# Block 0's second layer by unit halves, w_out in two transfers, and the transposing transfers one pair sooner in SyncE's queue

## The chip, the cores and the metric

The kernel runs on one core of a Trainium2 chip. The core has five engines with a queue of instructions each: PE (TensorE, matrix products and transposes), DVE (VectorE), ACT (ScalarE), POOL (GpSimd) and SP (SyncE, which here only issues transfers). Each queue is worked off in order, and an instruction that waits holds all that stand behind it. Sixteen DMA engines move data between HBM and SBUF. Matrix results land in PSUM, in eight banks. The metric is the time of one execution on the device in microseconds (us); lower is better. Shown are the median over several executions, and the profile of one of them.

## The reference

The input x has four sequences of 6144 tokens with 256 features. First a gated recurrence runs along each sequence, for each feature by itself:

```
f = lower_bound + (1 - lower_bound) * sigmoid(f_logit)
h[t] = f[t] * h[t-1] + (1 - f[t]) * x[t]
```

Then a layer works on each of the 24576 tokens, with the recurrence's output as its input h:

```
out = maximum(h @ w1, h @ w2) @ w_out        # w1, w2: 256 x 1024, w_out: 1024 x 256
```

All arrays are float32 outside. Inside, the kernel computes in float16 with float32 sums.

## The kernel before, in words

**What is computed.** With wd = w2 - w1 the maximum is h @ w1 + relu(h @ wd). So the first layer needs only h @ wd and a ReLU (`first_layer`, L434 and L442), and the part h @ w1 @ w_out is folded into one 256 x 256 matrix w13 = w1 @ w_out (`make_w13`, L390). The recurrence is run with u = 1 - sigmoid (ACT), and the factor 1 - lower_bound is folded into the weights. The second layer (`second_layer`, L480) sums ten products per group of 128 tokens: two with w13 and eight with w_out's 1024 units. From pair 2 on, two blocks are computed together by a scheme with seven products in place of eight (`sevenths`, L643), whose sums and differences DVE forms (L499), and whose results leave PSUM by ACT (L559) and DVE (L561) into the tile osb, and from there by SyncE's `store` to memory.

**Tiles and stages.** A block is 512 tokens. The first four blocks are chunks 0 to 3 by themselves; every later chunk has 1024 tokens and is a pair of blocks, so chunk c (c from 4) is pair c - 2, and the last is pair 23. The opening prepares the weights and blocks 0 to 3; then one loop runs over the pairs, sixteen slots each. In a slot TensorE computes one of a pair's sixteen first-layer units (two products of 512 columns) and nine or so products of the pair before. ACT and DVE meanwhile run the sigmoid (`pair_gate`, L279), the decay (L207), the product with x (L217) and the scan (L224) of the pair after.

**How a chunk comes in.** Features must lie on the partitions, and the types must be float16. `fetch` (POOL, L100) casts f_logit and x of a chunk from memory into a scratch array in memory, of which there are two for each. `cross` lets SyncE transpose them from scratch into SBUF (tiles fT and xT, four buffers each, L148), then lets POOL wait until fT has landed, with a copy of one element into `waited` (`pool_waits`, L341), and then fetches the next chunk. So cast, transpose, POOL's wait and the next cast follow one another. Blocks 0 to 3 come in without scratch and are transposed by TensorE (`first_turn`, L136; `turn`, L174).

**What sets the order.** The schedule is written out by hand: each engine's queue holds the instructions in the order in which the program makes them. In the opening, POOL's queue is: a wait for the first part of w1, the transfer of w_out into the tile wob (L666), then the inputs of chunks 1 to 4. TensorE's is: block 0's first layer, `make_w13`, the turning of block 1, and block 0's second layer in seven of eight slots with the turning of block 2 and the first layer of block 1 between. `cross(4)` stands before block 0's second layer, `cross(5)` behind block 1's, and in the loop, at slot 2 of pair p, stands the `cross` of pair p + 2. SyncE's queue therefore holds the transposes of chunk c, then the two stores of pair c - 5, then the transposes of chunk c + 1. The tile osb has four buffers, two per pair. PSUM has two double banks for the first layer (tile dT) and four for all else (tile ps).

In the profile, chunk 4's transposes are issued at 25.74 and 28.20 us, and the first product of pair 2 starts at 44.83 us.

Of the kernel before, what the change touches and what calls it, by code (L numbers as in the profile page):

```python
# [18 lines left out]
def kernel(  # L19
# [295 lines left out]
    lbr = const.tile([KC, P], FP32)  # L315
    waited = const.tile([P, 1], FP32)
    warm = const.tile([P, 1], FP32)
    wob = wpool.tile([P, FC, D], HALF)
    wd = wpool.tile([P, KC, DFF], HALF)
    w1T = wpool.tile([P, FC, D], HALF)  # L320
    w13 = wpool.tile([P, KC, D], HALF)
# [18 lines left out]
    def pool_waits(t):  # L340
        nc.gpsimd.tensor_copy(out=waited[:], in_=t)  # L341

    def scale_w1(g):
        for kc in range(KC):
            nc.scalar.mul(w1s[g][:, kc, :], w1n[g][:, kc, :], om[:, kc : kc + 1])

    def half_w1(g, copy):
        for kc in range(KC):
# [20 lines left out]
        g, q = divmod(fc, NQ)  # L369
        return slice(g * NQ * P + q, (g + 1) * NQ * P, NQ)  # L370

    def turn_w1(g):
        pt = ps_o.tile([P, NQ, KC, P], HALF, name="ps")
        for q in range(NQ):
            for kc in range(KC):
                nc.tensor.transpose(
                    pt[:, q, kc, :], w1h[g][:, kc, q : NQ * P : NQ], ident[:]
                )
        return pt
# [5 lines left out]
        )  # L385

    def make_w13(kc):
        psw = ps_o.tile([P, 2, D], FP32, name="ps")
        for fc in range(FC):
            nc.tensor.matmul(  # L390
                psw[:, 0, :],
                lhsT=w1T[:, fc, kc * P : (kc + 1) * P],
                rhs=wob[:, fc, :],
                start=(fc == 0),
                stop=(fc == FC - 1),
            )
        nc.scalar.copy(out=w13[:, kc, :], in_=psw[:, 0, :])

# [1 line left out]

    def right(k, cols):

        return wob[:, k * KH : (k + 1) * KH, cols], w13[:, k, cols]

    def make_sevens():
        b11, b12, b21, b22 = (right(k, c) for k in range(2) for c in (lo, hi))
# [19 lines left out]
    def first_layer(j, fc):  # L428
        k, g = divmod(fc, KH)
        if fc % 2 == 0:  # L430
            dts["d"] = ps_d.tile([P, 2, TB], FP32, name="dT")
        dT = dts["d"]
        for kc in range(KC):
            nc.tensor.matmul(  # L434
                dT[:, fc % 2, :],
                lhsT=wd[:, kc, unit_cols(fc)],
                rhs=y_of(j, kc),
                start=(kc == 0),
                stop=(kc == KC - 1),
            )  # L440
        if fc % 2:
            nc.scalar.activation(  # L442
                out=rts[j, k][:, g - 1 : g + 1, :].rearrange(
                    "p q (i m) -> p q i m", m=P
                ),
                in_=dT[:].rearrange("p q (m i) -> p q i m", m=P),
                func=AF.Relu,
            )

    def store(j, osb, groups=slice(0, TB // P), cols=slice(0, D), queue=None):  # L450
        b, t0, nb, c, o = blocks[j]
        r0 = b * S + t0
        (queue or nc.sync).dma_start(
            out=out[r0 : r0 + nb, :].rearrange("(p n) d -> p n d", p=P)[
                :, groups, cols
            ],
            in_=osb[:, groups, cols],
        )
# [3 lines left out]
    def second_layer(j, slot):  # L462
        ns = TB // P
        n = KC + FC
        total = ns * n
        for k in range(slot * total // FC, (slot + 1) * total // FC):
            i, s = divmod(k, n)
            g, r = divmod(i, 2)
            if s == 0 and r == 0:
                acc["ps"] = ps_o.tile([P, 2, D], FP32, name="ps")  # L470
                if i == 0:
                    acc["osb"] = opool.tile([P, TB // P, D], FP32, name="osb")
            ps, osb = acc["ps"], acc["osb"]
            toks = slice(i * P, (i + 1) * P)
            if s < KC:
                left, right = y_of(j, s)[:, i:TB:ns], w13[:, s, :]
            else:
                fc = s - KC
                left, right = rts[j, fc // KH][:, fc % KH, toks], wob[:, fc, :]
            nc.tensor.matmul(  # L480
                ps[:, r, :],
                lhsT=left,
                rhs=right,
                start=(s == 0 and r == 0),
                stop=(s == n - 1 and r == 1),
                skip_group_check=True,
            )
            if r == 1 and s == n - 1:
                (nc.scalar.copy if j in (0, 3) else nc.vector.tensor_copy)(
                    out=osb[:, 2 * g : 2 * g + 2, :], in_=ps[:]  # L490
                )
                if i == ns - 1:
                    store(j, osb)

    sums = {}

# [160 lines left out]
    with tc.manual_schedule():  # L657
# [4 lines left out]
        fetch_first(1)  # L662
        for g in range(NG):
            fetch_w(g)
        pool_waits(w1n[0][:, 0, 0:1])
        nc.gpsimd.dma_start(  # L666
            out=wob[:].rearrange("p (g q) c -> p g (q c)", g=NG),
            in_=moe_w_out.rearrange("(g p q) c -> p g (q c)", g=NG, q=NQ),
        )
        for c in range(1, 5):  # L670
            for s in range(2):
                fetch(c, s)
        wt = ps_d.tile([P, 2, 2 * TB], HALF, name="dT")
        lbc = ps_d.tile([P, TB], FP32, name="dT")

# [21 lines left out]
        first_turn(1, 0)  # L697
        first_turn(1, 1)
        first_recurrence(1)
        warm_up(24)  # L700
        scale_w1(0)
        half_w1(0, nc.scalar.copy)
        scale_w1(1)
        pt0 = turn_w1(0)
        for pair in range(2):
            make_wd(0, pair)
            for fc in range(2 * pair, 2 * pair + 2):
                first_layer(0, fc)
        half_w1(1, nc.vector.tensor_copy)
        pt1 = turn_w1(1)  # L710
        for pair in range(2):
            make_wd(1, pair)
            for fc in range(4 + 2 * pair, 6 + 2 * pair):
                first_layer(0, fc)
        keep_w1T(0, pt0)
        keep_w1T(1, pt1)
        steps = turn_steps(1)
        make_w13(0)
        turn(steps[:8])
        gate(1)  # L720
        make_w13(1)
        turn(steps[8:])
        for step in scan_steps(1):
            step()
        cross(4)
        for fc in range(FC):
            if fc == 4:
                turn(turn_steps(2))
                gate(2)
            if fc == 6:  # L730
                first_layer(1, 0)
                first_layer(1, 1)
            if fc < 7:
                second_layer(0, fc)
        for step in scan_steps(2):
            step()
        for step in make_sevens():
            step()
        for fc in range(2, FC):
            first_layer(1, fc)  # L740
            if fc == 3:
                second_layer(0, 7)
        turn(turn_steps(3))
        gate(3)
        early = scan_steps(3)
        for fc in range(FC):
            first_layer(2, fc)
            second_layer(1, fc)
            if fc < 4:
                early[fc]()  # L750
        cross(5)
        scans = {PAIR0: pair_scans(PAIR0)}
        gates = {0: 0, 1: 1, 4: 2, 5: 3}
        order = {
# [16 lines left out]
        for p in range(PAIR0, NPAIR):  # L771
            first = p == PAIR0
            more = p + 1 < NPAIR
            seq = [
                (27, scans[p]["scan10"]),
                (36, scans[p]["scan11"]),
                (112, lambda: sum3(p)),
            ]
            if more:
                scans[p + 1] = pair_scans(p + 1)  # L780
                seq += [
                    (64, scans[p + 1]["decay0"]),
                    (66, scans[p + 1]["drive0"]),
                    (70, scans[p + 1]["scan00"]),
                    (84, scans[p + 1]["scan01"]),
                    (131, scans[p + 1]["decay1"]),
                    (133, scans[p + 1]["drive1"]),
                ]
            if not first:
                seq += [  # L790
                    (9, lambda: sum1(p - 1)),
                    (18, lambda: sum2(p - 1)),
                    (50, lambda: sum4(p - 1)),
                ]
                queue += sevenths(p - 1)
            seq.sort(key=lambda e: e[0])
            gates = {4: 0, 6: 1, 12: 2, 14: 3} if more else {}
            for slot in range(2 * FC):
                first_layer(2 * p + slot // FC, slot % FC)
                if first and slot in pieces3 or p == PAIR0 + 1 and slot == 1:  # L800
                    second_layer(2 * PAIR0 - 1, piece)
                    piece += 1
                if p > PAIR0 + 1 or (p == PAIR0 + 1 and slot >= LAG):
                    due += NSEV / (2 * FC)
                    while due >= 1:
                        due -= 1
                        queue.pop(0)()
                if slot == 2 and p + 2 < NPAIR:
                    cross(blocks[2 * p + 4][3])
                if slot in gates:  # L810
                    pair_gate(p + 1, gates[slot])
                while seq and seq[0][0] < (slot + 1) * 9:
                    seq.pop(0)[1]()
# [38 lines left out]
```

## Time and profile before

| What | Before |
|---|---|
| Median of 4 executions | 380.51 us (378.33 to 380.92) |
| The profiled execution: its time, and its span in the profile | 380.78 us, 379.0 us |
| PE busy | 369.8 us, 98% of the span |
| DVE, ACT, POOL busy | 338.5, 303.2, 44.1 us |
| Granted TensorE clock | full throughout |
| Bytes moved | 77.17 MB, mean 204 GB/s |
| Cast into scratch: f, x, from issue to landing | 7.8, 10.2 us (median of 22 each) |
| Transposes of f, x, from issue to landing | 6.2, 5.0 us (median of 22 each) |
| Stores of 512 KB, from issue to landing | 4.4 us (median of 46) |

The busy shares say how much of the span an engine worked; matrix products overlap, so a busy PE is not one at its peak. The profile also gives the chain of work that ended last, followed back from the last instruction, and for each group of instructions the idle time of its engine just ahead, with what ended it. In the timeline a row is: start in us, length in us, engine (a q behind it is the engine's own sequencer, which issues transfers or waits), line, operation, output and inputs, count, and in brackets the idle time ahead and what ended it. In the windows a row has, for each engine, busy us and the number of instructions, then the TensorE clock, the DMA share and GB/s.

### The profile page before, as it was taken

What the parts mean: (1) busy time and instruction counts of PE and PEld (TensorE: products, weight loads), DVE (VectorE), ACT (ScalarE), POOL (GpSimd) and SP (SyncE); (2) the same over time, 40 slices, a digit from 0 to 9 for tenths busy, and PEclk for the clock granted to TensorE, in tenths of its full rate; (3) what the DMA queues carried; (4) which work ended last, traced back from release to release, by engine and by line L of the source; (5) the groups of instructions that cost most, each with busy time, mean ns of one, the idle gap of its engine ahead of it and who ended that gap; (6) DMA issues with size and microseconds to landing.
All of it is one profiled execution on the core that took longest, in us unless ns stands there. A gap on an engine that the chain in (4) does not pass through costs nothing.

```text
span 379.0 us, 9634 instructions
## 1 busy us (share of the span) xinstructions
PE 369.8 (98%) x4156; PEld 281.9 (74%) x4156; DVE 338.5 (89%) x408; ACT 303.2 (80%) x412; POOL 44.1 (12%) x80
## 2 busy tenths in 40 slices
PE   7899999999999999999999999999999999999995
PEld 6577767777777777777777777777777777777784
DVE  5796789999999999999999999999999899999762
ACT  4956798888888798888888888887987788889752
POOL 1501102102101011012012011010210110200000
PEclk9999999999999999999999999999999999999999
DMA  8999989999989899999999998997998988993223
GB/s 279 205 204 256 199 159 256 219 183 265 223 151 246 133 252 214 191 198 312 158 212 175 236 259 164 237 254 126 277 194 162 258 174 216 280 141 140 113 110 114
DMA packets 104543, 77.17 MB, mean 204 GB/s; under 512 B 93298, under 2 KB 95348, under 8 KB 103796
## 3 DMA queue, kind: packets, MB, share of 16 engines
q1 hardware_dynamic: 101536, 51.19, 59.0%
q0 software_dynamic: 2544, 25.17, 36.3%
q8 instruction: 32, 0.52, 0.6%
q10 hardware_dynamic: 420, 0.20, 0.2%
q14 instruction: 11, 0.09, 0.1%
HBM read 53.48 MB, written 48.23 MB: 268 GB/s over the span
## 4 chain that ended last, share of the span: by engine, by line
DMA 61%; PE 32%; POOL 2%; issue 2%; SPq 1%; ACT 1%; DVE 0%; POOLq 0%; DVEq 0%
DMA scr<-in_f_logit_dram 29%; DMA fT<-scr 28%; PE dT L434 14%; PE ps L643 13%; PE ps L480 5%; DMA xT<-in_x_dram 2%; POOL waited L341 2%; DMA r<-in_moe_w_dram 2%; PE ps L174 1%; SPq L117 0%; ACT r L442 0%; POOL wob L666 0%; DVE osb L561 0%; ACT u L279 0%; POOL fT L105 0%
## 5 line engine op out<-in xcount | busy, mean ns | idle before, releaser
L442 ACT ACTIVATE r<-dT 128x1024 f16<-128x1024 f32 x192 | 196.0, 1023 | 52.5 <-PE dT L434 52.3
L434 PE MATMUL dT<-r,wd 128*128 128x512 f16 x768 | 225.0, 379 | 0.7 <-ACT r L442 0.7
L643 PEld LDWEIGHTS <-S 128*128 128x128 f16 x1760 | 115.5, 101 | 37.2 <-DVE S L499 0.2
L643 PEld LDWEIGHTS <-r 128*128 128x128 f16 x1320 | 90.9, 101 | 36.9 <-issue 0.2
L224 DVE TENSOR_TENSOR_SCAN r<-ff,r,v 128x512 f16<-128x512 f16 x88 | 108.1, 1269 | 0.8
L643 PE MATMUL ps<-t,S 128*128 128x128 f16 x1320 | 101.6, 219 | 0.0
L499 DVE TENSOR_TENSOR S<-r 128x2560 f16<-128x2560 f16 x44 | 65.4, 1486 | 13.9 <-ACT r L442 13.9
L434 PEld LDWEIGHTS <-wd 128*128 128x128 f16 x768 | 67.7, 113 | 5.4 <-issue 0.8
L643 PE MATMUL ps<-wob,r 128*128 128x128 f16 x704 | 69.9, 219 | 0.0
L499 DVE TENSOR_TENSOR S<-r,S 128x2560 f16<-128x2560 f16 x44 | 64.9, 1474 | 0.0
L279 ACT ACTIVATE u<-fT 128x512 f16<-128x512 f16 x88 | 56.1, 638 | 1.8 <-DMA fT<-scr 1.8
L341 POOL CAST waited<-fT 128x1 f32<-128x1 f16 x22 | 18.3, 832 | 287.5 <-DMA fT<-scr 287.5
L207 DVE TENSOR_SCALAR ff<-u,nom 128x512 f16<-128x512 f16 (+1 forms) x98 | 31.8, 345 | 10.3 <-ACT u L279 4.4
L643 PE MATMUL ps<-w,r 128*128 128x128 f16 x176 | 38.5, 219 | 0.0
L643 PE MATMUL ps<-t,r 128*128 128x128 f16 x430 | 34.1, 219 | 0.1
L561 DVE TENSOR_TENSOR osb<-ps,sn 128x512 f32<-128x512 f32 x44 | 30.1, 684 | 3.2 <-PE ps L643 3.2
L643 PE MATMUL ps<-wob,S 128*128 128x128 f16 x352 | 32.6, 219 | 0.0
L217 DVE TENSOR_TENSOR v<-u,xT 128x1024 f16<-128x1024 f16 x44 | 30.1, 683 | 0.8 <-DMA xT<-scr 0.7
L549 ACT COPY sn<-ps 128x512 f32<-128x512 f32 x44 | 25.8, 587 | 2.0 <-PE ps L643 2.0
L559 ACT COPY osb<-ps 128x512 f32<-128x512 f32 x43 | 25.0, 582 | 0.8 <-PE ps L643 0.8
L480 PEld LDWEIGHTS <-r 128*128 128x128 f16 x160 | 16.0, 101 | 6.5
L643 PE MATMUL ps<-w,S 128*128 128x128 f16 x88 | 19.3, 219 | 0.0
(58 smaller groups left out, 136.3 us busy)
## 6 DMA issues: line engine op xcount, KB each, us to landing
out_dram<-osb SPq DMA_DIRECT2D x46, 512.0 KB, 4.4
scr<-in_f_logit_dram POOLq DMA_DIRECT2D x22, 512.0 KB, 7.8
scr<-in_x_dram POOLq DMA_DIRECT2D x22, 512.0 KB, 10.2
r<-in_moe_w_dram SPq DMA_DIRECT2D x4, 512.0 KB, 7.1
fT<-in_f_logit_dram POOLq DMA_DIRECT2D x3, 256.0 KB, 7.9
xT<-in_x_dram POOLq DMA_DIRECT2D x3, 256.0 KB, 8.7
out_dram<-osb SPq DMA_DIRECT2D x3, 256.0 KB, 2.5
osb<-in_f_logit_dram SPq DMA_DIRECT2D x2, 256.0 KB, 3.3
```

What stands on the lines that cost most here:

```text
L207: nc.vector.tensor_scalar(out=ff[:, h, cols], in0=u[:, h, cols], scalar1=nom[:, h : h + 1], scalar2=1.0, op0=ALU.mult, op1=ALU.add,)
L217: nc.vector.tensor_tensor(out=like(v[:, :, cols], xT), in0=like(u[:, :, cols], xT), in1=xT, op=ALU.mult,)
L224: nc.vector.tensor_tensor_scan(out=y_of(j, h), data0=ff[:, h, o : o + TB], data1=v[:, h, o : o + TB], initial=0.0 if t0 == 0 else y_of(j - ...
L279: nc.scalar.activation(out=mids[p + NBLK, "u"][:, h, cols], in_=held[c, 0][:, h, cols], func=AF.Sigmoid, scale=-1.0,)
L341: nc.gpsimd.tensor_copy(out=waited[:], in_=t)
L434: nc.tensor.matmul(dT[:, fc % 2, :], lhsT=wd[:, kc, unit_cols(fc)], rhs=y_of(j, kc), start=(kc == 0), stop=(kc == KC - 1),)
L442: nc.scalar.activation(out=rts[j, k][:, g - 1 : g + 1, :].rearrange("p q (i m) -> p q i m", m=P), in_=dT[:].rearrange("p q (m i) -> p q i ...
L480: nc.tensor.matmul(ps[:, r, :], lhsT=left, rhs=right, start=(s == 0 and r == 0), stop=(s == n - 1 and r == 1), skip_group_check=True,)
L499: nc.vector.tensor_tensor(out=t[:], in0=a, in1=b, op=op)
L549: nc.scalar.copy(out=t[:], in_=bank[b][:])
L561: nc.vector.tensor_tensor(out=dst, in0=bank[b][:], in1=snap[name][:], op=ALU.add)
L643: nc.tensor.matmul(bank[b][:, i, :], lhsT=a[:, k, cols], rhs=w, start=fresh, stop=after is not None, skip_group_check=True,)
```

## The change

There are two parts.

In the opening, w_out comes in two transfers into two tiles, one for each half of the 1024 units, and POOL's wait ahead of them is for block 0's last sigmoid. Block 0's second layer is split by unit halves (`second_first`): units 0 to 3 of all four token groups run right behind their first layer, ahead of the second half of w1's turning; the two terms with w13 and units 4 to 7 follow after `make_w13`. The second half of w1 is scaled by DVE in place of ACT. Block 0's last ReLU goes to DVE. w13's two halves share one PSUM tile of the first layer's pool. Block 2's transposes are split into those of f and those of x. Block 0's results leave by ACT as before, and block 3's too.

In the queue of SyncE, `cross` of each chunk from 5 on stands one block or pair sooner: `cross(5)` ahead of block 1's second layer, `cross(6)` behind it, and in the loop that of pair p + 3 at pair p. SyncE's queue then holds the transposes of chunk c and behind them the stores of pair c - 6.

```diff
-    wob = wpool.tile([P, FC, D], HALF)
+    wob = [wpool.tile([P, KH, D], HALF, name=f"wob{g}") for g in range(2)]
...
     def make_w13(kc):
-        psw = ps_o.tile([P, 2, D], FP32, name="ps")
+        if kc == 0:
+            dts["w"] = ps_d.tile([P, 2, TB], FP32, name="dT")
+        psw = dts["w"][:, kc, :]
...
+            if j == 0 and fc == FC - 1:
+                nc.vector.tensor_scalar_max(out=dst, in0=src, scalar1=0.0)
+            else:
+                nc.scalar.activation(out=dst, in_=src, func=AF.Relu)
...
+    def open_first():
+        acc["first"] = [ps_o.tile([P, 2, D], FP32, name="ps") for g in range(2)]
+        acc["osb0"] = opool.tile([P, TB // P, D], FP32, name="osb")
+
+    def second_first(i, fcs, y=False):
+        ns = TB // P
+        g, r = divmod(i, 2)
+        ps, osb = acc["first"][g], acc["osb0"]
+        toks = slice(i * P, (i + 1) * P)
+        terms = [(y_of(0, s)[:, i:TB:ns], w13[:, s, :]) for s in range(KC) if y]
+        terms += [
+            (rts[0, fc // KH][:, fc % KH, toks], wob[fc // KH][:, fc % KH, :])
+            for fc in fcs
+        ]
+        for n, (left, right) in enumerate(terms):
+            nc.tensor.matmul(
+                ps[:, r, :],
+                lhsT=left,
+                rhs=right,
+                start=(fcs[0] == 0 and r == 0 and n == 0),
+                stop=(fcs[-1] == FC - 1 and n == len(terms) - 1),
+                skip_group_check=True,
+            )
+        if fcs[-1] == FC - 1 and r == 1:
+            nc.scalar.copy(out=osb[:, 2 * g : 2 * g + 2, :], in_=ps[:])
+            if i == ns - 1:
+                store(0, osb)
...
-        pool_waits(w1n[0][:, 0, 0:1])
-        nc.gpsimd.dma_start(
-            out=wob[:].rearrange("p (g q) c -> p g (q c)", g=NG),
-            in_=moe_w_out.rearrange("(g p q) c -> p g (q c)", g=NG, q=NQ),
-        )
-        for c in range(1, 5):
-            for s in range(2):
-                fetch(c, s)
...
         first_recurrence(1)
+        pool_waits(mids[0, "u"][:, 0, TB - 1 : TB])
+        for g in range(NG):
+            nc.gpsimd.dma_start(
+                out=wob[g][:].rearrange("p q c -> p (q c)"),
+                in_=moe_w_out[g * NQ * P : (g + 1) * NQ * P, :].rearrange(
+                    "(p q) c -> p (q c)", q=NQ
+                ),
+            )
+        for c in range(1, 5):
+            for s in range(2):
+                fetch(c, s)
         warm_up(24)
-        scale_w1(0)
+        scale_w1(0, nc.scalar.mul)
         half_w1(0, nc.scalar.copy)
-        scale_w1(1)
         pt0 = turn_w1(0)
         for pair in range(2):
             make_wd(0, pair)
             for fc in range(2 * pair, 2 * pair + 2):
                 first_layer(0, fc)
+        keep_w1T(0, pt0)
+        scale_w1(1, nc.vector.tensor_scalar_mul)
         half_w1(1, nc.vector.tensor_copy)
-        pt1 = turn_w1(1)
+        pt1 = new_pt()
+        open_first()
+        for fcs in ((0, 1), (2, 3)):
+            for i in range(TB // P):
+                second_first(i, fcs)
+        turn_w1(1, pt1)
         for pair in range(2):
             make_wd(1, pair)
+            if pair:
+                keep_w1T(1, pt1)
             for fc in range(4 + 2 * pair, 6 + 2 * pair):
                 first_layer(0, fc)
-        keep_w1T(0, pt0)
-        keep_w1T(1, pt1)
         steps = turn_steps(1)
-        make_w13(0)
         turn(steps[:8])
         gate(1)
+        make_w13(0)
+        turn(steps[8:])
         make_w13(1)
-        turn(steps[8:])
         for step in scan_steps(1):
             step()
         cross(4)
-        for fc in range(FC):
-            if fc == 4:
-                turn(turn_steps(2))
-                gate(2)
-            if fc == 6:
-                first_layer(1, 0)
-                first_layer(1, 1)
-            if fc < 7:
-                second_layer(0, fc)
+        last = tuple(range(KH, FC))
+        for i in range(3):
+            second_first(i, last, True)
+        steps = turn_steps(2)
+        turn(steps[:8])
+        gate(2)
+        second_first(3, last, True)
+        first_layer(1, 0)
+        first_layer(1, 1)
+        turn(steps[8:])
         for step in scan_steps(2):
             step()
         for step in make_sevens():
             step()
         for fc in range(2, FC):
             first_layer(1, fc)
-            if fc == 3:
-                second_layer(0, 7)
         turn(turn_steps(3))
         gate(3)
+        cross(5)
         early = scan_steps(3)
         for fc in range(FC):
             first_layer(2, fc)
             second_layer(1, fc)
             if fc < 4:
                 early[fc]()
-        cross(5)
+        cross(6)
...
-                if slot == 2 and p + 2 < NPAIR:
-                    cross(blocks[2 * p + 4][3])
+                if slot == 2 and p + 3 < NPAIR:
+                    cross(blocks[2 * p + 6][3])
```

## The prediction

> **What bounds the kernel now.** I read the page's busy shares first, then the chain that ended last, then the queues of SP and POOL, then the opening microseconds.
>
> ```profile
> PE 369.8 (98%) x4156; PEld 281.9 (74%) x4156; DVE 338.5 (89%) x408; ACT 303.2 (80%) x412; POOL 44.1 (12%) x80
> ...
> DMA 61%; PE 32%; POOL 2%; issue 2%; SPq 1%; ACT 1%; DVE 0%; POOLq 0%; DVEq 0%
> DMA scr<-in_f_logit_dram 29%; DMA fT<-scr 28%; PE dT L434 14%; PE ps L643 13%; PE ps L480 5%; DMA xT<-in_x_dram 2%; POOL waited L341 2%; DMA r<-in_moe_w_dram 2%; PE ps L174 1%; SPq L117 0%; ACT r L442 0%; POOL wob L666 0%; DVE osb L561 0%; ACT u L279 0%; POOL fT L105 0%
> ```
>
> TensorE is busy 98% of the span, yet the chain runs through DMAs: cast f into scratch, transpose it into SBUF, let POOL see it, start the next cast. Both are true only if two bounds lie side by side. The waits of the SP queue and of POOL say that the DMA loop waits for nothing but itself:
>
> ```profile
> SPq L148 <- DMA scr<-in_f_logit_dram: 168.4, 21, 20.8
> ...
> POOL waited L341 <- DMA fT<-scr: 287.5, 22, 15.7
> ```
>
> The timeline of SP shows two turns of the loop:
>
> ```profile
> 79.13 4.12 SPq L148 DMA_TRANSPOSE fT<-scr  x1
> 83.34 2.85 SPq L148 DMA_TRANSPOSE xT<-scr  x1
> 86.30 1.51 SPq L453 DMA_DIRECT2D out_dram<-osb  x2
> 94.37 3.59 SPq L148 DMA_TRANSPOSE fT<-scr  x1
> 98.21 1.94 SPq L148 DMA_TRANSPOSE xT<-scr  x1
> 100.25 2.29 SPq L453 DMA_DIRECT2D out_dram<-osb  x2
> ```
>
> SP sits idle from 87.8 to 94.37, when the cast of chunk 9 lands. From chunk 8 (79.13) to chunk 25 (334.52) a turn takes 255.39/17 = 15.0 us. A pair of blocks takes TensorE 14.72 us (the sigmoids of successive chunks start at 74.68, 89.40, 104.12, 118.85). So the loop loses 0.3 us per pair against TensorE. In the trace the sigmoid of chunk 7 starts 3.1 us after its transpose landed, that of chunk 12 0.5 us, those of chunks 19 to 25 0.0 to 0.7 us. Once it costs TensorE something (timelines of ACT and PE):
>
> ```profile
> 287.45 0.58 ACT L559 COPY osb<-ps 128x512 f32<-128x512 f32 x1
> 297.14 0.63 ACT L279 ACTIVATE u<-fT 128x512 f16<-128x512 f16 x1 [1.52 <-DMA fT<-scr]
> 303.08 0.58 ACT L559 COPY osb<-ps 128x512 f32<-128x512 f32 x1
> ```
> ```profile
> 298.73 0.59 PE L434 MATMUL dT<-r,wd 128*128 128x512 f16 x2 [0.70 <-ACT r L442]
> ```
>
> The ReLU stands behind the late sigmoid on ACT. The two copies of successive pairs are 15.63 us apart instead of 14.72: 0.9 us lost, the one visible stall of the steady part. The opening is the other place (windows):
>
> ```profile
> 15.00:20.00 5.00, 4.15 (x43) 3.20 (x42) 2.10 (x5) 3.48 (x5) 0.49 (x1) 1.00 1.12 210
> 10.00:20.00 10.00, 8.51 (x76) 5.87 (x74) 6.63 (x16) 8.14 (x12) 4.97 (x9) 1.00 1.01 194
> ```
> ```profile
> 18.96 0.62 PE L174 MATMUL ps<-ident,xT 128*128 128x128 f16 x8 [0.85 <-DMA xT<-in_x_dram]
> ```
>
> TensorE idles 1.49 us of those ten, 0.85 us of it for block 1's x. From 20 us on it is full.
>
> **What the Trainium skill says.** "DMA: Bandwidth & Descriptors", section "Issuing engines are not separate DMA queues": DMAs of all issuers interleave on the same 16 engines. The trace agrees: a pair of stores issued before the next cast lands in 3.9 us (median, 251.2), a pair around its issue in 12.0 us:
>
> ```profile
> out_dram<-osb SPq DMA_DIRECT2D x2, 512.0 KB, 12.0
> scr<-in_f_logit_dram POOLq DMA_DIRECT2D x1, 512.0 KB, 8.9
> ```
>
> "SBUF — State Buffer", section "Who interferes with whom": a DVE operation in a 2-port mode locks GpSimd out; this touches the moved POOL wait and its DMA issues. The traced one-element POOL copies take 0.18 to 1.32 us, so something holds them. "VectorE: DVE Perf Modes", section "The perf-mode tier table": fp32 tensor_scalar in SBUF runs at 2x, PSUM fp32 at 1x.
>
> **Part 1, the opening.** The matmuls are the same (40 of 256 columns for block 0's second layer); only order and engines change. POOL now waits for block 0's second sigmoid (ends 7.82) instead of w1 (9.04). Copy 0.2 to 0.65; wob's issue starts near 8.4 instead of 9.63. Two issues at 0.55 (the fT row's price) replace one of 0.87: chunk 1's issue is about 1.0 us earlier, and the whole POOL stream with it. First half of wob: its packets then share the engines with the weights until about 12, so I put its landing at 13.3 (bounds 12.8 and 14.5).
>
> TensorE, from rows of the timeline (8 transposes 0.43, 8 matmuls of 256 columns 0.86, 8 of 512 1.71): first-layer units 0-3 end at 13.74 as now; the second ReLU ends at 14.85. Second layer with units 0-3, 16 matmuls, from 13.95 to 15.75. Second w1 half: DVE does wd (to 12.01), keep (0.64), two scalings (fp32 tensor_scalar, unseen; 0.43 like the fp32 cast, at most 0.68), two casts (0.86), so it is ready at 14.4 to 14.9, hidden behind those 16 matmuls. Transposes to 16.2, units 4-7 to 17.9. Then fT of block 1 to 18.3, w13 first half to 19.2, xT to 19.65 (x lands near 18 now: its wait is gone). But w13's halves now share one PSUM tile, and ACT has the sigmoid (1.02) before the first w13 copy: copy ends 19.8, second half to 20.7, copy to 21.15, and only then the second term of the remaining second layer. That is 0.2 + 0.4 us idle. The last ReLU on DVE (unseen; 1024 fp32 from PSUM, 1.2 us by the 1.22 us of the drive, bounds 1.0 to 1.4) ends at 19.2 and is hidden by w13. Remaining: 23 matmuls 2.46, block 2's transposes 0.86, block 1's first layer 3.41, block 3's transposes 0.86; ACT's ReLUs (1.02 each against 0.86 on TensorE) add about 0.5. Block 2's first layer starts near 29.4; the DVE chain gives 29.5. Now it starts at 28.97. So **+0.4 us**, bounds -1.5 (all opening idleness filled) and +1.2 (wob late).
>
> **Part 2, the queue.** SP's order becomes f, x of chunk c, then the stores of pair c-6 instead of c-5. The transposes wait for their casts, so moving them cannot start them sooner by itself. The chain gains only what no longer lies beside it: the earlier POOL stream (about 1.0 us, bounds 0 and 1.2); block 1's store at 37.77, now behind chunk 5's transposes (fT took 7.3 us to land, without it some 6: 1.3, plus 0.3 of SP's wait); at chunk 8 one store beside the loop instead of two (one turn with two took 14.7 us for cast and transpose, chunk 7's with one 11.3; I count 1.4). Sum g = 4.0 us of lead, bounds 1 and 6. Any g over 1.5 removes the 0.9 us stall: **-0.9 us**.
>
> The price is behind the waiting transposes: each store leaves one turn, 14.7 us, later, and holds its osb buffer; there are four, two per pair. The stores after chunk c's transposes must land before pair c-4 first writes. With today's landing times and g = 0 the worst is chunk 21: issued 280.33 and 280.95, landed 291.6 and 293.7, needed at 287.45 (ACT) and 288.99 (DVE): 4.1 and 4.7 us late. With g = 4 that is 0.1 and 0.7, within what ACT can absorb (at 297 an ACT gap of 1.52 cost TensorE 0.70, so about 0.8). All others are earlier. So **0**, bounds 0 and +3.9.
>
> The inp buffers add no wait: chunk c takes that of chunk c-4, whose last sigmoid ran more than 20 us before.
>
> Sum against the execution shown: 379.0 + 0.4 - 0.9 + 0 = 378.5 us span, 1.78 around it, 380.3 for its 380.78. The median of the runs is 380.51, so 380.0.
>
> **Rivals.**
> A (0.40), as summed: 380.0. Its own range is 378.7 to 382.3, within 0.5% (1.9 us, about what a measurement of this kernel can tell from no change).
>
> B (0.31), faster: the opening fills its 1.49 us idle and the chain's lead takes the 0.9 us, 380.5 - 2.4 = 378.1. For it: the four runs reach down to 378.33, so an undisturbed loop may be worth more than the one visible stall. Against: TensorE's sum above meets new waits at w13.
>
> C (0.22), slower: SyncE's stores come too late. With g = 1 the worst lateness is 3.7, less 0.8 absorbed, 2.9; with -0.9 + 0.4 it gives +2.4, 382.9, and 383.9 at g = 0. It decides below g = 1.5 or when stores land later than 12.7 us after issue. For it: in 9 of the 18 pairs of stores between 70 and 330 us at least one now takes over 10 us. Against: the lead of part 2.
>
> D (0.07): wob's first half lands at 14.5 or later, or POOL is held by DVE: TensorE waits at the first second-layer matmul, and the ACT order adds its share, +2 us, 382.5.
>
> That the transposes do not start sooner at all is contained in C: then g is the POOL stream alone.
>
> **The numbers.** Faster by over 0.5% 0.31 (B), within 0.40 (A), slower 0.29 (C, D). The range: 377.4 below B (0.7 for what the other runs suggest), 383.5 inside C.
>
> **What would show it.** Right: no ACT wait for fT after 100 us; fT landing 4 us or more ahead of its sigmoid; leave copies 14.72 apart throughout; block 2's first layer starting at 29 to 30; SP's stores about 14 us after their copies. Wrong: ACT or DVE at the leaves (L559, L561 of now) waiting for a store's DMA; a wait for wob at 14; the first f transpose not before 25.5; block 2's first layer before 28.3.

## The result, and the profile after

| | Before | After |
|---|---|---|
| Median | 378.95 us (64 runs, 377.93 to 382.73, and one of 429.01) | 380.13 us (43 runs, 379.31 to 381.79) |
| The profiled execution: time, span | 380.78 us, 379.0 us | 380.13 us, 378.4 us |
| PE busy | 369.8 us, 98% | 368.3 us, 97% |
| DVE, ACT, POOL busy | 338.5, 303.2, 44.1 us | 340.2, 301.0, 37.8 us |

The changed kernel takes 1.003 of the time before, 95% interval 1.002 to 1.0039: it is 1.2 us slower. The forecast time was 380.0, and 380.13 was measured; the forecast direction was wrong. The cause of that shows in the first row. The four runs shown ahead of the prediction had a median of 380.51 us. The 64 runs that the comparison now holds, those four among them, have 378.95, and only 9 of them lie at 380.2 or above, three of the four among these nine. In three later comparisons the same kernel had 378.87, 379.06 and 379.06.

The page of after, its busy shares, the chain that ended last by engine and by line, and the sigmoids:

```profile
PE 368.3 (97%) x4156; PEld 280.4 (74%) x4156; DVE 340.2 (90%) x411; ACT 301.0 (80%) x409; POOL 37.8 (10%) x81
...
PE 94%; DMA 3%; ACT 1%; SPq 0%; issue 0%; DVE 0%; POOL 0%; DVEq 0%
PE ps L677 45%; PE dT L439 43%; PE ps L484 3%; DMA wob<-in_moe_w_out_dram 2%; PE ps L516 1%; DMA osb<-in_x_dram 1%; PE ps L174 1%; SPq L117 0%; PE dT L395 0%; ACT r L452 0%; ACT u L201 0%; DVE osb L595 0%; ACT w L402 0%; ACT u L252 0%; DVE osb L616 0%
...
L279 ACT ACTIVATE u<-fT 128x512 f16<-128x512 f16 x88 | 56.0, 637 | 0.0
```

The chain has left the DMA loop: 94% of it is TensorE, where in the profile of before 61% was DMA. The 1.8 us that the sigmoids waited for fT are 0.0. But neither is the change's doing alone: two more profiles of the kernel before (below) have 94% and 96% of TensorE in the chain and no such wait. The page of the last of them:

```profile
PE 96%; DMA 1%; ACT 1%; SPq 0%; DVE 0%; issue 0%; DVEq 0%
```

The waits of the SP queue and of POOL (total us, times, longest) nevertheless look almost as they did (168.4 and 287.5 before):

```profile
SPq L148 <- DMA scr<-in_f_logit_dram: 167.6, 22, 20.3
...
POOL waited L341 <- DMA fT<-scr: 278.4, 22, 16.5
```

So the size of these two waits does not tell what sets the end; the loop now runs ahead of TensorE. The timeline of SP after, chunks 8 and 9:

```profile
76.72 4.43 SPq L148 DMA_TRANSPOSE fT<-scr  x1
81.25 2.08 SPq L148 DMA_TRANSPOSE xT<-scr  x1
83.44 0.99 SPq L457 DMA_DIRECT2D out_dram<-osb  x2
91.79 2.82 SPq L148 DMA_TRANSPOSE fT<-scr  x1
94.71 2.81 SPq L148 DMA_TRANSPOSE xT<-scr  x1
97.62 0.99 SPq L457 DMA_DIRECT2D out_dram<-osb  x2
```

Chunk 8's transpose is issued at 76.72 instead of 79.13, and chunk 25's at 318.69 instead of 334.52, so that a turn of the loop takes (318.69 - 76.72)/17 = 14.2 us instead of 15.0. Its lead over TensorE, the time from the landing of a chunk's fT to the first sigmoid that reads it, grows from 6.1 us at chunk 8 to 12 to 14 us at the end. The leave copies of the place where before lost 0.9 us (timeline of ACT after) are 14.72 apart again:

```profile
287.72 0.58 ACT L593 COPY osb<-ps 128x512 f32<-128x512 f32 x1
...
302.44 0.58 ACT L593 COPY osb<-ps 128x512 f32<-128x512 f32 x1
```

The loss is in the opening, as the experiments below show. Its timeline on TensorE:

```profile
13.75 1.91 PE L516 MATMUL ps<-wob,r 128*128 128x256 f16 x16 [0.48 <-DMA wob<-in_moe_w_out_dram]
...
18.11 1.04 PE L395 MATMUL dT<-wob,w1T 128*128 128x256 f16 x8
18.99 0.61 PE L174 MATMUL ps<-ident,xT 128*128 128x128 f16 x8
19.65 1.03 PE L395 MATMUL dT<-wob,w1T 128*128 128x256 f16 x8
20.52 0.27 PE L516 MATMUL ps<-w,r 128*128 128x256 f16 x1
21.14 0.27 PE L516 MATMUL ps<-w,r 128*128 128x256 f16 x1 [0.35 <-ACT w L402]
...
27.55 1.02 PE L439 MATMUL dT<-r,wd 128*128 128x512 f16 x4 [0.25 <-ACT r L452]
29.30 0.59 PE L439 MATMUL dT<-r,wd 128*128 128x512 f16 x2
```

A start-to-start reading shows more than the brackets, since ends are modelled: eight products of 256 columns take 0.86 us and eight transposes 0.43. TensorE loses 0.64 us before 13.75 (wob), 0.22 before 19.65 and 0.52 around 20.52 to 21.14 (w13), and 0.41 before 27.55 (ReLU). The line at 29.30 is block 2's first layer; before had it at 29.03 in the profile read for the prediction. The timeline of ACT shows what holds w13: the sigmoid in front of the first copy, and the second copy behind the second half's products.

```profile
18.31 1.02 ACT L201 ACTIVATE u<-ps 128x1024 f16<-128x1024 f16 x1 [0.29 <-PE ps L174]
19.23 0.37 ACT L402 CAST w<-dT 128x256 f16<-128x256 f32 x1
...
20.72 0.37 ACT L402 CAST w<-dT 128x256 f16<-128x256 f32 x1 [1.12 <-PE dT L395]
```

### The profile page after: what moved, and what is told of

The parts are those of the page before. It is cut to its first block, busy times and chain, and to the rows that moved or that the text cites. A ratio compares the mean times of both kernels' runs of the same rounds, so it can differ in the third digit from the quotient of the medians.

```text
span 378.4 us, 9635 instructions
## 1 busy us (share of the span) xinstructions
PE 368.3 (97%) x4156; PEld 280.4 (74%) x4156; DVE 340.2 (90%) x411; ACT 301.0 (80%) x409; POOL 37.8 (10%) x81
## 4 chain that ended last, share of the span: by engine, by line
PE 94%; DMA 3%; ACT 1%; SPq 0%; issue 0%; DVE 0%; POOL 0%; DVEq 0%
PE ps L677 45%; PE dT L439 43%; PE ps L484 3%; DMA wob<-in_moe_w_out_dram 2%; PE ps L516 1%; DMA osb<-in_x_dram 1%; PE ps L174 1%; SPq L117 0%; PE dT L395 0%; ACT r L452 0%; ACT u L201 0%; DVE osb L595 0%; ACT w L402 0%; ACT u L252 0%; DVE osb L616 0%
## 5 line engine op out<-in xcount | busy, mean ns | idle before, releaser
L677 PEld LDWEIGHTS <-r 128*128 128x128 f16 x1320 | 90.9, 101 | 36.8 <-issue 0.2
L341 POOL CAST waited<-fT 128x1 f32<-128x1 f16 x22 | 11.2, 510 | 278.4 <-DMA fT<-scr 278.4
L484 PEld LDWEIGHTS <-r 128*128 128x128 f16 x120 | 12.1, 101 | 5.8
```

Of the source, the lines that this page charges most:

```text
L484: nc.tensor.matmul(ps[:, r, :], lhsT=left, rhs=right, start=(s == 0 and r == 0), stop=(s == n - 1 and r == 1), skip_group_check=True,)
L677: nc.tensor.matmul(bank[b][:, i, :], lhsT=a[:, k, cols], rhs=w, start=fresh, stop=after is not None, skip_group_check=True,)
```

## The experiments

Two quantities are read from every profile. The **opening** runs from block 0's first product with wd to that of block 2; its idle time is its length less the columns of its products and transposes at the rates just given (15.91 us of work), so that it also holds what the products lose without a visible wait. The **rest** runs from block 3's first product with wd to the end of the span; between the two lie 7.82 us in every profile but two, told of below.

### The kernel before again, and each half of the change alone

First the kernel before, unchanged, for a second profile.

> The kernel before, unchanged, for a second profile. Theory T1 (the execution profiled first was an unlucky one: its fT stall of 0.9 us and its wait of 0.85 us for block 1's x are not typical): span near 377.2 us, block 2's first layer starts near 28.2 us instead of 29.03, no gap in TensorE near 300 us. Rival T2 (that execution was typical in its phases, and the change costs time in the steady part in a way that one profile doesn't show): the same waits again, 0.85 us at the x of block 1 and at least one TensorE gap of 0.5 us or more after 100 us.

The queue alone, on the kernel before:

```diff
         gate(3)
+        cross(5)
         early = scan_steps(3)
...
-        cross(5)
+        cross(6)
...
-                if slot == 2 and p + 2 < NPAIR:
-                    cross(blocks[2 * p + 4][3])
+                if slot == 2 and p + 3 < NPAIR:
+                    cross(blocks[2 * p + 6][3])
```

> Only the queue part: the kernel before, with the cross of each chunk from 5 on one block or pair sooner. T1 (the loss is all in the opening): ratio 0.996 to 1.000, because the steady part loses its stalls and the opening is as before; fT lands 4 us or more ahead of its sigmoid after 100 us. T2 (the loss is in the later stores): ratio 1.002 to 1.004, with waits for a store's landing at the copies into osb.

The opening alone, on the changed kernel:

```diff
         gate(3)
-        cross(5)
         early = scan_steps(3)
...
-        cross(6)
+        cross(5)
...
-                if slot == 2 and p + 3 < NPAIR:
-                    cross(blocks[2 * p + 6][3])
+                if slot == 2 and p + 2 < NPAIR:
+                    cross(blocks[2 * p + 4][3])
```

> Only the opening part: the changed kernel, with the crosses at their old places. T1: ratio 1.002 to 1.006, block 2's first layer starting at 29 us or later; the steady part as in the kernel before, with fT landing 0 to 4 us ahead of its sigmoid. T2: ratio 0.998 to 1.001, because the opening costs what it saves.

The queue, and of the opening only POOL's order, on the kernel before (w_out in one DMA):

```diff
-        pool_waits(w1n[0][:, 0, 0:1])
-        nc.gpsimd.dma_start(
...
         first_recurrence(1)
+        pool_waits(mids[0, "u"][:, 0, TB - 1 : TB])
+        nc.gpsimd.dma_start(
...
(and the lines of the queue alone)
```

> The kernel before with the queue part, and of the opening part only POOL's wait on block 0's second sigmoid in place of w1 (w_out still one transfer, the order of TensorE, ACT and DVE as before). T1: the earlier stream of POOL brings block 1's x about 1 us sooner, which takes the wait of up to 0.85 us in front of its transposes away; ratio 0.994 to 0.999, at or below that of the queue part alone. Rival T3 (the earlier stream of w_out takes bandwidth from w1 and w2, and so the opening's first products come later): ratio 0.3% or more above the queue part alone, with the first transposes of w1 starting later than 10.9 us.

Measured (us; ratio to the kernel before, with its 95% interval):

| | Median | Ratio | Opening (profile) | idle in it | Rest |
|---|---|---|---|---|---|
| before, shown first | | | 17.18 | 1.27 | 342.15 |
| before, again (one run, 379.29) | | | 17.37 | 1.46 | 341.23 |
| after | 380.13 | 1.0030 (1.0020 to 1.0039) | 17.92 | 2.01 | 341.24 |
| the queue alone | 378.66 | 0.9988 (0.9969 to 1.0006) | 17.94 | 2.03 | 341.23 |
| the opening alone | 380.72 | 1.0034 (1.0013 to 1.0055) | 17.80 | 1.89 | 341.63 |
| queue and POOL's order | 378.95 | 0.9991 (0.9972 to 1.0009) | 17.75 | 1.84 | 341.24 |

The rest takes 341.2 us whether the transposes stand ahead of the stores or behind them (the third profile of before, below, has 341.26). The 342.15 of the profile read for the prediction is the exception: its 0.9 us stall was not there when the same kernel was profiled again. So the queue has little to repair. It does lengthen the lead, and the opening alone shows what is left without it, twice in its whole profile (timeline of ACT):

```profile
179.27 0.63 ACT L279 ACTIVATE u<-fT 128x512 f16<-128x512 f16 x1 [0.81 <-DMA fT<-scr]
```

Its rest is 0.4 us longer than the others', and these two stalls are what its trace shows for it. The opening alone is as slow as both parts together (1.0034 against 1.0030), so the loss is the opening's. The ratios put the opening at +1.3 us (0.5 to 2.1) and the queue at -0.5 (-1.2 to +0.2). POOL's order is not what costs it: added to the queue's edit, it measured like the kernel before, within its interval. Nor did it take the wait for block 1's x away, as was expected of it. The timeline of TensorE there:

```profile
18.56 0.62 PE L174 MATMUL ps<-ident,xT 128*128 128x128 f16 x8 [0.78 <-DMA xT<-in_x_dram]
```

A single profile of the opening does not say this. The queue alone has the opening of the kernel before, yet 2.03 us idle in it, because wob landed at 16.68 that time; its profiled execution was also the slowest of its 22 runs (380.29 against a median of 378.66). A third profile of the kernel before was therefore taken later.

> The kernel before, unchanged, for a third profile. T1 (its waits in the opening are for DMA landings and differ from run to run): a wait for w_out, for block 1's f or for block 1's x or none of them, their sum other than 1.0 us by 0.2 or more; no TensorE gap of 0.5 us or more after 30 us. T2: a TensorE gap of 0.5 us or more after 100 us, as in the first profile.

It took 378.38 us. The timeline of TensorE in the opening, with no idle time in brackets in this stretch:

```profile
11.00 2.05 PE L434 MATMUL dT<-r,wd 128*128 128x512 f16 x8
...
15.14 1.06 PE L390 MATMUL ps<-wob,w1T 128*128 128x256 f16 x8
16.05 0.61 PE L174 MATMUL ps<-ident,fT 128*128 128x128 f16 x8
16.49 1.04 PE L390 MATMUL ps<-wob,w1T 128*128 128x256 f16 x8
17.36 0.61 PE L174 MATMUL ps<-ident,xT 128*128 128x128 f16 x8
17.81 0.49 PE L480 MATMUL ps<-w,r 128*128 128x256 f16 x2
...
27.52 0.59 PE L434 MATMUL dT<-r,wd 128*128 128x512 f16 x2
```

The opening takes 16.52 us with 0.61 idle, and no wait for a DMA is in it: wob landed at 14.48, ahead of the 15.14 at which it is first read, and x of block 1 was there at 17.36. So the kernel before has an opening of 16.5 us when its transfers come in time, and neither the 0.85 us wait for x nor the 0.9 us stall that the prediction gave to the change is there every time. Some wait for a transfer is common, though: of the five profiles with TensorE's old order two wait for x, two for wob and fT, and only this one for none. The start of the opening moves as well: in the three profiles of before it lies at 11.85, 11.11 and 11.00 us, with the first weights landed at 8.99, 8.24 and 8.14. Against 16.52 the changed opening is 1.4 us longer.

The medians give an estimate of the usual run, if the rest is alike in all runs. Of a time, some 1.8 us lie around the span, 341.2 are the rest and 7.82 lie between. For before that puts block 2's first layer at 378.95 - 350.8 = 28.1 us (the three profiles have 29.03, 28.47, 27.52), for after at 380.13 - 350.8 = 29.3 (its profile has 29.30).

### Which wait of the new opening

Four edits on the changed kernel, from one comparison. First, w13's halves in a PSUM tile each, and the products with w13 last in the remaining second layer:

```diff
-        if kc == 0:
-            dts["w"] = ps_d.tile([P, 2, TB], FP32, name="dT")
+        dts["w"] = ps_d.tile([P, 2, TB], FP32, name="dT")
...
-        terms = [(y_of(0, s)[:, i:TB:ns], w13[:, s, :]) for s in range(KC) if y]
-        terms += [
+        terms = [
             (rts[0, fc // KH][:, fc % KH, toks], wob[fc // KH][:, fc % KH, :])
             for fc in fcs
         ]
+        terms += [(y_of(0, s)[:, i:TB:ns], w13[:, s, :]) for s in range(KC) if y]
```

> The changed kernel with the waits for w13 taken away: in block 0's last products the terms with w_out come ahead of the two with w13, and each half of w13 has its own PSUM tile. T1 (the opening costs three waits of TensorE that the other order didn't have: w_out 0.64, w13 0.22 + 0.52, ReLU 0.41 us): 0.6 to 0.75 us less than the changed kernel, ratio to the kernel before 1.001 to 1.002; no wait for the copies of w13 is left. Rival T4 (these waits only fill time in which ACT and DVE are late anyway, so they come back as a longer wait for the ReLU before block 2): within 0.2 us of the changed kernel, ratio 1.0025 to 1.0035, and the ReLU wait near 27.5 us grows from 0.41 to about 1 us.

That, and block 0's second pair of token groups copied out by DVE in place of ACT, to free ACT for the ReLUs near 27.5 us:

```diff
-            nc.scalar.copy(out=osb[:, 2 * g : 2 * g + 2, :], in_=ps[:])
+            (nc.vector.tensor_copy if g else nc.scalar.copy)(
+                out=osb[:, 2 * g : 2 * g + 2, :], in_=ps[:]
+            )
```

> As the kernel without the waits for w13, and the second half of block 0's results leaves PSUM by DVE in place of ACT, so that ACT is free for block 1's first ReLU 0.58 us sooner. T1: the ReLU wait of 0.41 us goes as well, about 1.1 us less than the changed kernel, ratio 0.9995 to 1.001. T4: DVE becomes the bound at block 2's scans, which end 0.6 us later: no gain over the kernel without the waits for w13.

The changed kernel with POOL's old wait:

```diff
-        pool_waits(mids[0, "u"][:, 0, TB - 1 : TB])
+        pool_waits(w1n[0][:, 0, 0:1])
```

> The changed kernel with POOL's wait for the first part of w1 as before, so that w_out is issued about 0.9 us later. T5 (the packets of the cast transfers come only when the engines are done with the weights, near 10.5 us, however early they are issued): w_out's first half lands within 0.4 us of the 13.71 us in the changed kernel, ratio 1.002 to 1.004. Rival T6 (landing follows the issue one to one): lands near 14.6 us, the wait for it grows by 0.9 us, ratio 1.0045 to 1.006.

And, on the second of these edits, the second halves of w1 and w2 fetched only behind wob's first half (the memset makes the fetch wait for POOL):

```diff
-        for g in range(NG):
-            fetch_w(g)
+        fetch_w(0)
...
+            if g == 0:
+                nc.gpsimd.memset(w1n[1][:, 0, 0:1], 0.0)
+                fetch_w(1)
```

> As the kernel with the w13 waits and the ReLU wait taken away, and the second halves of w1 and w2 are issued by SyncE only after w_out's first half is issued by POOL (a one-element write of POOL into the second w1 tile holds them back). T5: w_out's first half then lands before 13.2 us and its wait of 0.5 to 0.64 us goes; the second half of w1 lands 1.0 to 1.5 us later, near 12.5, just in time; ratio 0.998 to 1.000, below both kernels if the steady part keeps its lead. T6: the weights' second half comes later than DVE needs it and the wait moves there: ratio as without this step or 0.1 to 0.3% above.

| | Median | Ratio | Opening (profile) | idle in it | Rest |
|---|---|---|---|---|---|
| w13's order | 379.38 | 1.0005 (0.9987 to 1.0023) | 17.86 | 1.95 | 341.22 |
| and DVE's copy | 379.46 | 1.0008 (0.9989 to 1.0028) | 17.19 | 1.28 | 341.22 |
| POOL's old wait | 379.94 | 1.0025 (1.0012 to 1.0038) | 17.93 | 2.02 | 341.22 |
| w1 and w2 behind wob | 385.87 | 1.0163 (1.0129 to 1.0197) | 22.18 | 6.27 | 341.22 |

**w13.** With its order changed, TensorE's timeline has only 0.08 us left of the 0.74 lost at w13:

```profile
14.44 1.91 PE L515 MATMUL ps<-wob,r 128*128 128x256 f16 x16 [1.07 <-DMA wob<-in_moe_w_out_dram]
...
20.12 1.04 PE L394 MATMUL dT<-wob,w1T 128*128 128x256 f16 x8
21.00 0.60 PE L515 MATMUL ps<-wob,r 128*128 128x256 f16 x4
21.43 0.46 PE L515 MATMUL ps<-w,r 128*128 128x256 f16 x2
```

The opening of this profile is no shorter, because wob's wait came out at 1.23 us this time instead of 0.64. In the medians the edit shows: 379.38 against after's 380.13, and against 379.94 of the kernel that differs from after by POOL's wait alone and ran beside it; six of the edit's 14 runs lie below the lowest of that kernel's 22. So w13 costs 0.6 to 0.75 us of the 1.2. Which of the edit's two steps, the tiles or the order, gives how much was not run.

**POOL's new wait.** It is worth little. The timelines of POOL, and then the DMA issues (count, KB each, median us from issue to landing), after first:

```profile
7.71 1.22 POOL L728 DMA_DIRECT2D wob<-in_moe_w_out_dram  x2
```
```profile
wob<-in_moe_w_out_dram POOLq DMA_DIRECT2D x2, 256.0 KB, 6.3
```

and with POOL's old wait:

```profile
8.55 1.22 POOL L728 DMA_DIRECT2D wob<-in_moe_w_out_dram  x2
```
```profile
wob<-in_moe_w_out_dram POOLq DMA_DIRECT2D x2, 256.0 KB, 5.2
```

Issued 0.84 us later, the halves took 1.1 us less, and the first landed at 13.47 instead of 13.71; the weights ahead of it had landed 0.2 us sooner in that execution. What holds it is on the engines: from 8.5 to 10 us no packet of POOL's queue moves in either trace, while those of SyncE's weights keep the engines busy (DMA share 1.05); POOL's begin at 10.6 and 10.3 us and have the engines nearly to themselves from 11.5 us on. The Trainium skill, "DMA: Bandwidth & Descriptors", section "Issuing engines are not separate DMA queues", has transfers of all issuers on the same sixteen engines, interleaved. These two runs agree that the engines are shared, but the two streams interleave only as the weights run out, and an earlier issue buys no earlier landing while they last.

**Weights behind wob.** The other way round it is worse. Here wob's first half was issued at 7.95, its packets moved from 9.3 us on, and it landed at 11.80. But the second half of w1, issued at 8.78, then landed at 14.85 and that of w2 at 18.6, where the kernel before has them at 11.5 and 12.5. DVE's timeline shows both as waits:

```profile
14.95 0.88 DVE L345 TENSOR_SCALAR r<-r,om 128x512 f32<-128x512 f32 x2 [2.47 <-DMA r<-in_moe_w_dram]
...
18.63 1.67 DVE L358 SCALAR_TENSOR_TENSOR wd<-r,om 128x256 f16<-128x256 f32 x4 [2.13 <-DMA r<-in_moe_w_dram]
```

**The ReLUs.** DVE's copy did not remove the wait at 0.41 us. Timeline of ACT with that edit:

```profile
24.26 1.02 ACT L451 ACTIVATE r<-dT 128x1024 f16<-128x1024 f32 x1 [0.45 <-PE dT L438]
25.57 1.94 ACT L451 ACTIVATE r<-dT 128x1024 f16<-128x1024 f32 x2 [0.29 <-PE dT L438]
```

ACT now even waits for TensorE first, and TensorE is held all the same. A ReLU takes 1.02 us, the four products of a unit pair 0.86, and there are two dT buffers: three pairs in a row cannot be read as fast as they are made. An earlier start of ACT does not change that.

### Two attempts on the ReLU's wait and on wob's

Block 1's first layer was interleaved with block 3's turning, on the kernel with w13's order, to give ACT time between ReLUs. And, on top of it, the second half of w2 alone was held behind wob's first half:

```diff
+        steps = turn_steps(3)
         for fc in range(2, FC):
             first_layer(1, fc)
-        turn(turn_steps(3))
+            if fc == 3:
+                turn(steps[:8])
+            if fc == 5:
+                turn(steps[8:])
```

> As the kernel without the waits for w13, and block 3's transposes are put between the units of block 1's first layer, so that TensorE has other work while ACT runs the ReLUs. T1 (the ReLU wait of 0.41 us is a lack of other work on TensorE there, since a ReLU of 1.02 us follows products of 0.86 us): the wait goes, 0.3 to 0.4 us less, ratio 0.999 to 1.0005, so that the opening costs no more than the one before. Rival T4 (ACT is the bound up to block 3's sigmoid, and the wait only moves behind block 1's first layer): block 2's first layer starts no sooner after block 0's first layer than without this step (17.2 us or more), ratio as without this step.

```diff
-        for g in range(NG):
-            fetch_w(g)
+        fetch_w(0)
+        fetch_w(1, (0,))
...
+            if g == 0:
+                nc.gpsimd.memset(w2n[1][:, 0, 0:1], 0.0)
+                fetch_w(1, (1,))
```

> As the kernel before this one, and only w2's second half is issued behind w_out's first half (w1's second half stays ahead). T1: w_out's first half lands near 12.8 us, its wait of 0.4 to 0.6 us becomes 0 to 0.1; w2's second half lands near 14 us, and DVE's second difference of weights starts at most 1 us later, covered by the 16 products of the second layer; ratio 0.9975 to 0.9995, below the kernel before. T6 (a weight transfer issued behind the cast stream lands as late as w2's second half did when both were held back, near 18.6 us): the wait moves to the second difference of weights, ratio 1.006 or more.

Measured: 379.24 us, ratio 1.0005 (0.9992 to 1.0018), and 380.48 us, 1.0044 (1.0027 to 1.0060). The interleaving removes the wait for the ReLU but gains nothing that can be measured against w13's order alone (1.0005 too): the recurrence on DVE, whose scans now arrive last, makes TensorE wait at 30.34, and from block 2's to block 3's first layer it takes 8.09 us instead of 7.82, in both of these profiles. (The opening of the interleaved version's profile, 17.91 us, is not shorter; it holds the half rate told of in the last section.) Holding w2 back makes it slower, with the same sort of late weight:

```profile
16.11 1.67 DVE L358 SCALAR_TENSOR_TENSOR wd<-r,om 128x256 f16<-128x256 f32 x4 [1.59 <-DMA r<-in_moe_w_dram]
```

No version was clearly faster than the kernel before. The lowest median is the queue alone, 378.66 beside 378.87 in the same comparison, with an interval that includes 1.

## Why the prediction was wrong

**The step that failed** is the last of the sum, "The median of the runs is 380.51, so 380.0", with the two terms in front of it, "+0.4" and "-0.9". Both were measured on one execution, and the sum took that execution, and the four runs around it, as the state of the kernel before. Its stall of 0.9 us and its 0.85 us wait for x do not come every time: neither was in the second or the third profile (the second waits for wob and fT in its opening instead, 0.66 and 0.43 us), and the median of the same kernel lies 1.8 us below that execution. What comes every time is the cost on the other side of the sum. "+0.4" was counted against an opening with a DMA wait of nearly a microsecond in it (17.18 us long); against 16.52 us it is +1.4, the medians say +1.2, and the opening alone measured +1.3 (0.5 to 2.1). The queue alone measured -0.5 (-1.2 to +0.2), an interval that holds both -0.9 and nothing; that it has nothing to take away in most executions rests on the two other profiles.

For the execution shown the sum came out, 378.5 us of span forecast and 378.4 measured, but partly by luck. The changed opening took 17.92 us, where the forecast left it 29.4 - 11.85 = 17.55, and it started at 11.38 instead of 11.85, because the weights landed 0.5 us sooner. The kernel before has landings as early in its other profiles, so the change is not the reason. (The sum also has block 2's first layer of before at 28.97; the trace has 29.03.)

Rival B's argument pointed at the sign: "the four runs reach down to 378.33, so an undisturbed loop may be worth more than the one visible stall". It was used as a reason why the change might gain more, though it told equally that before often has no stall to remove.

**The opening, piece by piece.** Block 2's first layer starts at 29.30 (29.4 forecast). w13 idles 0.22 and 0.52 (0.2 and 0.4), by the sigmoid ahead of the copy as described, and taking it away gave the time back. This wait is steady: its bracket is 0.35 us in all three profiles that have it (after, the opening alone, POOL's old wait). The ReLUs cost 0.41 (0.5). DVE's two scalings took 0.88 together (0.43 each was put); its ReLU out of PSUM took 1.23 (1.2). The x wait is gone. Two terms were too kind: wob's first half landed at 13.71, within the bounds but not at 13.3, a wait of 0.64; and "chunk 1's issue is about 1.0 us earlier, and the whole POOL stream with it" holds for the issue alone. The landing with POOL's old wait was no later, and chunk 4's first transpose, at 25.74 before and 25.24 after, came at 24.82 with POOL's old wait.

Together: the fixed waits of the new order are 0.74 + 0.41 = 1.15 us, and 0.64 of wob stands beside whatever wait for transfers the old order meets. Of the 1.2 us in the medians w13 is shown (0.6 to 0.75). The interleaving took the ReLU's 0.41 away without a measurable gain, so its share is not shown; wob's could not be taken away without a loss elsewhere, so its share is only read from the trace. What each adds to the remaining half microsecond stays open. The split of w_out into two transfers and DVE's scaling and ReLU were not run alone.

**The queue.** The first test held throughout: no sigmoid waits for fT after 100 us, copies 14.72 apart. The lead at chunk 8 grew from 2.55 to 6.13 us, by 3.6 (g = 4.0). The sum took the loop's turn as otherwise unchanged. In this profile it shortened, from 15.0 to 14.2 us, so the lead went on growing; with the queue alone it ended at 7.5 us. The price of later stores was 0, as put: the pair of copies at 70.31 and 72.42 was stored at 83.44 and 84.05, 11 to 13 us after, and no copy into osb waited for a store. That disposes of rival C as the cause, though the time it named is on the right side. Rival D named the right place, "TensorE waits at the first second-layer matmul, and the ACT order adds its share", but with wob's first half landing at 14.5 or later (13.71 measured); the ACT order was the larger part.

## What to carry to other kernels

Before the removal of a wait is credited, see whether it is in more than one execution: a DMA that lands late once is not a cost of the kernel, while a wait that follows from the order of instructions on an engine is there every time. A new order that trades the first kind for the second loses in the usual run, even where the sum against one profile comes out even. Set the sum against the fastest executions as well as the one profiled, and do not count an earlier DMA issue as an earlier landing while the engines are full.

## What was not expected of the hardware

In some profiles TensorE's products in the opening run at half rate for a while. In that of the interleaved version TensorE waited before its transposes, and the products behind ran at half rate. Its timeline, then the windows of the same stretch (PE and the other engines busy, then the granted clock, DMA share and GB/s):

```profile
10.70 0.25 PE L379 MATMUL ps<-ident,S 128*128 128x128 f16 x1 [1.81 <-ACT S L349]
...
11.94 3.16 PE L438 MATMUL dT<-r,wd 128*128 128x512 f16 x8
```
```profile
11.50:13.00 1.50, 1.50 (x10) 0.90 (x8) 1.10 (x3) 0.00 (x0) 0.47 (x1) 0.50 1.11 213
13.00:14.50 1.50, 1.50 (x5) 0.46 (x3) 1.50 (x5) 0.60 (x1) 0.25 (x1) 0.50 1.12 212
14.50:16.00 1.50, 1.50 (x11) 0.81 (x9) 1.42 (x4) 1.28 (x2) 0.76 (x2) 1.00 1.12 209
```

Products of 512 columns took 0.43 us instead of 0.21, for about 2.6 us, with a granted clock of 0.50. With the weights behind wob the same followed a gap of 2.04 us; after a gap of 1.62 us in the profile of after it did not. The Trainium skill, "TensorE: Matmul & The Clock Gate", section "Part 1: The HAM clock gate", describes a gate that goes to half rate after an idle window of about 3.4 us; the gaps here were shorter. That the gap is the cause is not shown: with w2 held back, the first products ran as slowly although TensorE had been at work since 8.31 us, and there the recorded clock was 1.00 (timeline of TensorE):

```profile
11.72 2.96 PE L438 MATMUL dT<-r,wd 128*128 128x512 f16 x8
```

It is one more reason why one profile of the opening does not speak for all.
